# A new order of all engines for retention and a squared-ReLU MLP: other durations in the plan, and two casts moved to ScalarE

## The chip, the cores and the metric

The kernel runs on one core of one Trainium2 chip. The metric is the device time of one execution, in microseconds. The median of eight executions of the kernel before is 289.78 us (289.51 to 290.66).

## What is computed

```
scores = q @ k^T / 8                      # 8 batches, 8 heads, 576 positions, head size 64
Dmat[i, j] = gamma_h ** (i - j) if i >= j else 0,  gamma_h = 1 - 2 ** (-5 - h)
x = (scores * Dmat) @ v                   # retention; x as 4608 tokens x 512
out = relu(x @ w_in) ** 2 @ w_out         # w_in 512 x 2048, w_out 2048 x 512; float32 in and out
```

## The kernel before

**Units and groups.** The 4608 tokens are 36 units of 128. Units 0 to 7 are pairs: two neighbouring units are loaded together (tile `pair`, one transfer for each of k, q, v) and handled by `add_unit_pair` and `add_ret_pair`; the others by `add_unit` and the joined retention code. Two units make a group, and there are 18 groups, 0 to 17.

**Retention.** It is done chunk by chunk with a state R. For a pair, k and q are cast to 16 bits (`kx`, `qx`, line 424) and v is multiplied by decay factors (`vx`, line 420), each in two halves; TensorE transposes kx and qx (`psT`, line 439), ScalarE copies the result (`kqT`, line 450). Then come small 64 x 64 matmuls on TensorE (line 357): scores (`psc`), k times v (`psS`) and outputs (`psO`). VectorE masks the scores (`rx`, line 490; `rT`, line 692 for later units), steps the state (`stmp`, `R`, lines 514 and 461) and scales the output into the MLP's input (`xT`, lines 577 and 751). Later units are cast by GpSimd (`kq`, `v`, lines 371 to 387) and transposed by a DMA that SP issues (line 400). psO2 below is the psO of group 2.

**MLP.** For each group, eight blocks of `ph` (line 876, 256 columns, 8 matmuls a block); ScalarE takes the ReLU (`rl`, line 884); ScalarE or VectorE squares it (`gT`, lines 894 and 896). The second layer of groups 1 to 17 is a Strassen product: seven products p1 to p7 of eight matmuls (`po`, line 973) instead of eight, from sums of gT (`gS`, line 946, VectorE) and sums of w_out (`wT`, line 827, VectorE). p1 and p2 need gT alone; p7, p6, p5 and p3 need sums, called here by number: sum 3 for p7, sum 2 for p6 (made in two halves), sum 1 for p5, sum 4 for p3; p4 needs wT3 and gT. Products share banks, so ScalarE copies p1, u2 and u4 out between them (line 986) and VectorE adds into `o` (line 996). Group 0 uses the plain product with 512 columns (line 916).

**The weights** come in eight transfers that GpSimd issues with a cast on the way (w0 to w3 of w_in, w4 to w7 of w_out), between the loads of pairs 0 and 2 and those of pairs 4 and 6. Before the first MLP block, TensorE runs 34 junk matmuls (`warm`, line 256) where it has nothing else.

**What sets the order.** Nothing is ordered by hand. Each piece of work is a task with an engine, a key and a duration; `Schedule.emit` plays them against each other, and each engine takes the ready task with the lowest key. The order that comes out is the program; on the chip semaphores hold each instruction until its inputs are there. The planned durations and landings so decide only the order, not the times. Transfers are tasks too, with a landing time of `after` plus an entry of `LAG`.

The line numbers in the text are those of the kernel before.

Of the kernel before, what the change touches and what calls it, by code (L numbers as in the profile page):

```python
# [15 lines left out]
class Schedule:  # L16
# [4 lines left out]
        self.count = dict(count)  # L21
        self.tasks = []

    def add(self, eng, key, dur, fn, deps=(), acq=(), after=None, lag=0.0):
        t = dict(eng=eng, key=key, dur=dur, fn=fn, acq=acq, n=len(self.tasks), users=[], free=[], lag=lag,
                 left=len(deps), ready=0.0, lat=self.LAT[eng] if after is None else after)
        for d in deps:
            d["users"].append(t)
        self.tasks.append(t)
        return t  # L30
# [11 lines left out]
    def emit(self):  # L42
        ready = {e: [] for e in self.LAT}
        busy = {e: False for e in self.LAT}
        events = []
        order = []
        seq = 0

        def push(at, what, t):
            nonlocal seq  # L50
            seq += 1
            heapq.heappush(events, (at, seq, what, t))
        for t in self.tasks:
            if t["left"] == 0:
                heapq.heappush(ready[t["eng"]], (t["key"], t["n"], t))
        now = 0.0
        while True:
            for e in ready:
                if busy[e]:
                    continue  # L60
                held = []
                while ready[e]:
                    item = heapq.heappop(ready[e])
                    t = item[2]
                    if all(self.count[r] >= t["acq"].count(r) for r in t["acq"]):
                        for r in t["acq"]:
                            self.count[r] -= 1
                        t["start"] = now
                        order.append(t)
                        busy[e] = True  # L70
                        push(now + t["dur"], "end", t)
                        break
                    held.append(item)
                for item in held:
                    heapq.heappush(ready[e], item)
            if not events:
                break
            now = events[0][0]
            while events and events[0][0] <= now + 1e-9:
                _, _, what, t = heapq.heappop(events)  # L80
                if what == "end":
                    busy[t["eng"]] = False
                    for w in t["users"]:

                        push(now + (0.0 if w["eng"] == t["eng"] else t["lat"]), "dep", w)
                    for g in t["free"]:
                        push(now + t["lat"], "free", g)
                elif what == "dep":
                    t["left"] -= 1
                    if t["left"] == 0:  # L90
                        push(now + t["lag"], "go", t)
                elif what == "go":
                    heapq.heappush(ready[t["eng"]], (t["key"], t["n"], t))
                else:
                    t["left"] -= 1
                    if t["left"] == 0:
                        self.count[t["res"]] += 1
        assert len(order) == len(self.tasks)
        for t in order:
            t["fn"]()  # L100
# [3 lines left out]
def kernel(  # L104
# [114 lines left out]
    for hp in range(NP):  # L219
# [2 lines left out]
    nc.scalar.activation(out=dec128, in_=lnrow_R, func=ACTF.Exp, scale=128.0)  # L222

    L = 2 * NF
    WARM = 34
    EARLY = 20
    SQ_ACT = (0, 1, 2, 3, 4, 5, 6)
    SPREAD = 0.1
    QL = 0.8
    BESIDE = 1.1  # L230
    PAUSE = 1.5
    PARTS = 1
    WT_KEY = 96
    URGENT = 40
    SQ_LATE = (1, 4, 6)
    JOIN = 5
    LAG = {"k4": 0.7, "q4": 0.5}
    LAG_T, LAG_O = 1.5, 5.0
    PAIRED = 8
    FIRST = ["k0", "q0", "v0", "k2", "q2", "v2", "w0", "w1", "w2", "w3", "w4", "w5", "w6", "w7", "k4", "q4", "v4", "k6", "q6", "v6"]  # L240
# [1 line left out]
                          R=5, Rm=2, kqT=6))  # L242
    add = sched.add
# [28 lines left out]
        nc.gpsimd.tensor_copy(out=iota_pt[0:64], in_=iota_p[0:64])  # L272
        nc.gpsimd.tensor_scalar(out=iota_pt[64:128], in0=iota_p[64:128], scalar1=-64.0, scalar2=None, op0=ALU.add)

    tail_pool = add_gated("POOL", 4, "v", 2.2, make_tail_pool)
    tail_dec = add("DVE", 0, 0.3, lambda: make_vdec("tail", tile_of["iota_pt"]), deps=[tail_pool])

    def dma_task(key, dur, fn, **kw):
# [46 lines left out]
    def add_weight(i):  # L325
        fb = i % 4

        def fn():
            src, dst = ((w_in[:, fb * 512:(fb + 1) * 512].rearrange("(m p) f -> p m f", p=P), w_in16[:, :, fb * 512:(fb + 1) * 512]) if i < 4 else
                        (w_out[fb * 512:(fb + 1) * 512, :].rearrange("(n p) m -> p n m", p=P), w_out16[:, fb * 4:(fb + 1) * 4, :]))  # L330
            tile_of["w", i] = nc.gpsimd.dma_start(out=dst, in_=src)  # L331
            if i == 0:
                behind(tile_of["w", i], tile_of["load", "v", 0])
        issue = add("POOL", -90 + i, 0.9, fn, deps=issues[-1:] or [loaded["v", 0]], lag=1.0 if issues else 0.0)
        issues.append(issue)
        t = add("SP", 0, 2.75, lambda: None, deps=last_load + [issue], after=2.1 + LAG.get(f"w{i}", 0.0))
        last_load[:] = [t]
        wcast[i] = [t]

# [63 lines left out]
    def add_unit_pair(u, base):  # L403
# [4 lines left out]
        for i, name in enumerate("kqv"):  # L408
            xs[name] = []
            for e in range(2):  # L410
                eng = ("DVE" if (e if name == "v" else lead) else "ACT" if name == "k" and u >= 4 or u == 2 and e else
                       "DVE" if name == "q" and u == 2 else "POOL")

                def fc(name=name, e=e, eng=eng):
                    if (name + "x", u) not in tile_of:
                        tile_of[name + "x", u] = cast.tile([P, 2, H * D], FP16, name=name + "x", tag="kq16")
                    t = tile_of[name + "x", u][:, e]
                    x = tile_of[name + "32", u][:, :, e * D:(e + 1) * D]
                    if name == "v":
                        (nc.vector if eng == "DVE" else nc.gpsimd).tensor_tensor(  # L420
                            out=t.rearrange("p (h d) -> p h d", d=D), in0=x,
                            in1=vdec[f"pair{e}"].rearrange("p (h o) -> p h o", o=1).to_broadcast([P, H, D]), op=ALU.mult)
                    else:
                        engines[eng](out=t.rearrange("p (n b a d) -> p n b a d", n=2, b=2, a=2),
                                     in_=x.rearrange("p (a n b) d -> p n b a d", n=2, a=2))
                dur = (dict(POOL=1.1, DVE=0.6) if name == "v" else dict(POOL=0.62, DVE=0.4, ACT=0.59))[eng]
                xs[name].append(add(eng, base + (7 if name == "v" else i + e / 2), dur, fc, deps=[loaded[name, u]],
                                    acq=() if e else ("kq",)))
            if xs[name][0]["eng"] == xs[name][1]["eng"]:
                sched.need(xs[name][1], xs[name][0])  # L430
# [270 lines left out]
    def after_sums(g, t, key, res):  # L701
# [21 lines left out]
        if not c0:  # L723
            T["Rread", g - 1].append(r0)
        r1 = add("DVE", key + 0.2 - URGENT, 0.69, fr1, deps=[r0])
        r2 = add("DVE", key + 0.3, 0.65, fr2, deps=[r1], acq=("R",))
        T["Rm", g], T["R", g], T["Rread", g], T["Rmread", g] = r0, r2, [], r1
        sched.free("ff", [r0])
        sched.free("ff", [r1])
# [92 lines left out]
    def add_wT(i, in0, in1):  # L822
        ts = []
        for h in range(2):
            def f(h=h):
                sl = slice(h * HF // 2, (h + 1) * HF // 2)
                nc.vector.tensor_tensor(out=wT[i][:, sl], in0=in0[:, sl], in1=in1[:, sl], op=ALU.subtract)
            ts.append(add("DVE", WT_KEY + i, 0.7, f, deps=sum((wcast[j] for j in range(4, 8 if i else 6)), [])))
        return ts

    t1 = add_wT(0, wB[0, 1], wB[0, 0])
# [1 line left out]
    t3 = add_wT(2, wB[1, 1], wB[0, 1])  # L833
    t4 = add_wT(3, wB[1, 0], wT[1])
    for x, y in ((t2, t1), (t4, t2)):
        for p in y:
            for w in x:
                sched.need(w, p)
    wT_done = {7: t3, 6: t2, 5: t1, 4: t4}

    def store(u, o, lo=0, hi=DM, engs=(nc.sync, nc.sync)):
# [16 lines left out]
    def add_ff(g):  # L858
# [10 lines left out]
        for fb in range(NF // nf):  # L869
# [18 lines left out]
            def fg(fb=fb, on_act=on_act):  # L888
# [5 lines left out]
                    nc.scalar.activation(out=t, in_=rl, func=ACTF.Square)  # L894
                else:
                    nc.vector.tensor_tensor(out=t, in0=rl, in1=rl, op=ALU.mult)  # L896
            r = add("ACT", place(4 * fb + 4), 0.6, fr, deps=[f1[-1]], acq=("rl",))
            sched.free("ff", [r])
            sq.append(add("ACT" if on_act else "DVE", place(4 * fb + 6), 0.63 if on_act else 0.55, fg, deps=[r] + sq[:1],
                          acq=() if fb else ("g",)))  # L900
            sched.free("rl", [sq[-1]])
        sched.free("x", [f1[-1]])
        base2 = base + NF * n
# [28 lines left out]
    def add_strassen(g, us, base, sq):  # L932
# [7 lines left out]
        def add_sum(k, key, parts, in0, in1, op, deps, start=()):  # L940
            out_ = []
            for h in range(parts):
                def f(sl=cut(parts, h)):
                    if ("S", g) not in tile_of:
                        tile_of["S", g] = stage.tile([P, 4, HF, P], FP16, name="gS", tag="wst")
                    nc.vector.tensor_tensor(out=tile_of["S", g][:, k, sl], in0=in0(sl), in1=in1(sl), op=op)  # L946
                out_.append(add("DVE", key + h, (BESIDE if h else 0.5) if parts > 1 else 0.8, f, deps=deps(h, parts) + list(start)))
            sums[k] = out_
            return out_
        nb = len(sq) // 2  # L950
# [161 lines left out]
```

## Time and profile before

| What | Value |
| --- | --- |
| profiled execution, its own time | 289.7 us |
| its span | 288.0 us |
| TensorE busy | 280.4 us (97%), 4346 matmuls |
| VectorE busy | 176.1 us (61%) |
| ScalarE busy | 187.6 us (65%) |
| GpSimd busy | 89.2 us (31%) |
| granted TensorE clock | 0.999 |
| share of TensorE in the chain that ended last | 91% |

A busy share is an average over the span. TensorE's rows are pipelined and their ends modelled: where two rows of one engine overlap, the starts are the firmer numbers, and the time that work took is read from start to start. Idle time of an engine that is not the bottleneck costs nothing.

### The profile page before, as it was taken

What the parts mean: (1) busy time and instruction counts of PE and PEld (TensorE: products, weight loads), DVE (VectorE), ACT (ScalarE), POOL (GpSimd) and SP (SyncE); (2) the same over time, 40 slices, a digit from 0 to 9 for tenths busy, and PEclk for the clock granted to TensorE, in tenths of its full rate; (3) what the DMA queues carried; (4) which work ended last, traced back from release to release, by engine and by line L of the source; (5) the groups of instructions that cost most, each with busy time, mean ns of one, the idle gap of its engine ahead of it and who ended that gap; (6) DMA issues with size and microseconds to landing.
All of it is one profiled execution on the core that took longest, in us unless ns stands there. A gap on an engine that the chain in (4) does not pass through costs nothing.

```text
span 288.0 us, 10135 instructions
## 1 busy us (share of the span) xinstructions
PE 280.4 (97%) x4346; PEld 235.9 (82%) x4346; DVE 176.1 (61%) x341; ACT 187.6 (65%) x363; POOL 89.2 (31%) x124
## 2 busy tenths in 40 slices
PE   6999999999999999999999999999999999999994
PEld 2568767888888888888888888888888888888883
DVE  4772389868566756647656564767565566364632
ACT  5558975667585857657576748675848675847830
POOL 5660035435524243433426151524434000000000
PEclk9999999999999999999999999999999999999999
DMA  7999999889998898989899997989889420102004
GB/s 200 276 208 207 247 292 269 162 235 161 219 223 172 217 207 206 182 209 163 222 150 231 205 196 166 210 201 238 185 195 210 96 77 2 73 2 75 0 4 144
DMA packets 122156, 49.94 MB, mean 173 GB/s; under 512 B 94720, under 2 KB 117760, under 8 KB 122112
## 3 DMA queue, kind: packets, MB, share of 16 engines
q1 hardware_dynamic: 117568, 44.84, 70.9%
q0 software_dynamic: 4224, 4.19, 8.8%
q8 instruction: 34, 0.56, 0.8%
q10 hardware_dynamic: 320, 0.26, 0.4%
q14 instruction: 10, 0.08, 0.1%
HBM read 36.70 MB, written 9.44 MB: 160 GB/s over the span
## 4 chain that ended last, share of the span: by engine, by line
PE 91%; DMA 3%; POOL 2%; issue 2%; DVE 0%; POOLq 0%; DVEq 0%
PE ph L876 44%; PE po L973 37%; PE psO L357 4%; DMA w_in<-in_moe_w_in_dram 3%; PE po L916 2%; PE psc L357 2%; PE psS L357 2%; PE psT L439 1%; POOL mask L216 0%; POOL vx L420 0%; POOL w_in L331 0%; DVE o L996 0%; POOL mask_full L208 0%; POOL mask_tail L208 0%; DVE p L1025 0%
## 5 line engine op out<-in xcount | busy, mean ns | idle before, releaser
L876 PE MATMUL ph<-xT,w_in 128*128 128x256 f16 x1152 | 136.6, 273 | 0.2 <-DMA w_in<-in_moe_w_in_dram 0.2
L876 PEld LDWEIGHTS <-w_in 128*128 128x128 f16 x1152 | 111.4, 98 | 14.6 <-DMA w_in<-in_moe_w_in_dram 0.5
L884 ACT ACTIVATE rl<-ph 128x512 f16<-128x512 f32 x144 | 84.3, 587 | 50.4 <-PE ph L876 47.8
L894 ACT ACTIVATE gT<-rl 128x512 f16<-128x512 f16 x118 | 74.4, 631 | 3.4
L973 PEld LDWEIGHTS <-gS 128*128 128x128 f16 x544 | 51.7, 98 | 6.5
L973 PE MATMUL po<-wT,gS 128*128 128x256 f16 x408 | 55.8, 273 | 0.0
L946 DVE TENSOR_TENSOR gS<-gT,gS 128x512 f16<-128x512 f16 (+1 forms) x51 | 30.7, 603 | 24.2 <-ACT gT L894 23.7
L973 PEld LDWEIGHTS <-gT 128*128 128x128 f16 x408 | 39.6, 98 | 4.9
L973 PE MATMUL po<-w_out,gT 128*128 128x256 f16 x272 | 36.7, 273 | 0.0
L387 POOL TENSOR_TENSOR v<-v,vdec_full 128x512 f16<-128x512 f32 x24 | 26.8, 1117 | 26.3 <-DMA v<-in_v_dram 13.8
L371 POOL CAST kq<-k 128x512 f16<-128x512 f32 x28 | 20.9, 748 | 35.0 <-DMA k<-in_k_dram 34.6
L946 DVE TENSOR_TENSOR gS<-gT 128x1024 f16<-128x1024 f16 x34 | 23.6, 695 | 7.0 <-ACT gT L894 6.9
L382 POOL CAST kq<-q 128x512 f16<-128x512 f32 x24 | 16.4, 685 | 32.7 <-DMA q<-in_q_dram 32.6
L896 DVE TENSOR_TENSOR gT<-rl 128x512 f16<-128x512 f16 x26 | 11.9, 457 | 20.7 <-ACT rl L884 20.7
L996 DVE TENSOR_TENSOR o<-po,u 128x256 f32<-128x256 f32 x33 | 13.9, 423 | 15.4 <-PE po L973 7.7
L986 ACT COPY u<-po 128x256 f32<-128x256 f32 x34 | 12.5, 369 | 15.8 <-PE po L973 15.7
L996 DVE TENSOR_TENSOR o<-po,p 128x256 f32<-128x256 f32 x18 | 7.6, 424 | 21.3 <-ACT u L986 13.4
L751 DVE TENSOR_TENSOR xT<-psO,gam_full 128x512 f16<-128x512 f32 x28 | 18.0, 685 | 4.0 <-PE psO L357 3.9
L973 PE MATMUL po<-w_out,gS 128*128 128x256 f16 x136 | 18.0, 273 | 0.0
L973 PE MATMUL po<-wT,gT 128*128 128x256 f16 x136 | 17.6, 273 | 0.0
L692 DVE TENSOR_TENSOR rT<-psc,mask_full 128x512 f16<-128x512 f32 x24 | 15.6, 685 | 3.1 <-PE psc L357 2.8
L461 DVE TENSOR_TENSOR R<-stmp,dec 128x512 f16<-128x512 f32 (+1 forms) x18 | 12.6, 702 | 0.5
(82 smaller groups left out, 219.9 us busy)
## 6 DMA issues: line engine op xcount, KB each, us to landing
out_dram<-o SPq DMA_DIRECT2D x32, 256.0 KB, 2.6
k<-in_k_dram SPq DMA_DIRECT2D x24, 256.0 KB, 4.3
q<-in_q_dram SPq DMA_DIRECT2D x96, 64.0 KB, 3.3
v<-in_v_dram SPq DMA_DIRECT2D x24, 256.0 KB, 3.4
pair<-in_k_dram SPq DMA_DIRECT2D x4, 512.0 KB, 7.1
pair<-in_q_dram SPq DMA_DIRECT2D x4, 512.0 KB, 7.3
pair<-in_v_dram SPq DMA_DIRECT2D x4, 512.0 KB, 6.9
w_in<-in_moe_w_in_dram POOLq DMA_DIRECT2D x4, 512.0 KB, 9.1
```

The source lines that it names most:

```text
L357: t = nc.tensor.matmul(out_, lhsT=lhsT, rhs=rhs, start=start, stop=True, skip_group_check=True, tile_position=(64 * row, 64 * col))
L371: op(out=out_.rearrange("p (n b a d) -> p n b a d", n=2, b=2, a=2), in_=in_.rearrange("p (a n b) d -> p n b a d", n=2, a=2))
L382: nc.gpsimd.tensor_copy(out=tile_of["kq", u][:, 1].rearrange("p (t a d) -> p a t d", t=4, a=2), in_=tile_of["q32", u].rearrange("p (a t) d ...
L387: nc.gpsimd.tensor_tensor(out=t, in0=tile_of["v32", u], in1=vdec[kind].rearrange("p (h o) -> p h o", o=1).to_broadcast([P, H, D]), op=ALU. ...
L692: tile_of["masking", g] = nc.vector.tensor_tensor(out=tile_of["rT", g][:, :, a], in0=tile_of["psc", g][a].rearrange("p (s n i) -> p s n i" ...
L751: nc.vector.tensor_tensor(out=tile_of["x", g].rearrange("p n (s e i) -> p e (n s) i", s=n, e=2)[:, c], in0=y.rearrange("p (o t r) -> p o r ...
L876: nc.tensor.matmul(tile_of["ph", g, fb][:, j, :], lhsT=w_in16[:, m, fi * P:(fi + 1) * P], rhs=tile_of["x", g][:, m, :], start=(m == 0), st ...
L884: nc.scalar.activation(out=t, in_=tile_of["ph", g, fb], func=ACTF.Relu)
L894: nc.scalar.activation(out=t, in_=rl, func=ACTF.Square)
L946: nc.vector.tensor_tensor(out=tile_of["S", g][:, k, sl], in0=in0(sl), in1=in1(sl), op=op)
L973: nc.tensor.matmul(tile_of["pb", g, bank], lhsT=left(i), rhs=right[:, i, :], start=(start and i == 0), stop=(i == HF - 1), skip_group_chec ...
L996: nc.vector.tensor_tensor(out=o_tile(u)[:, half * HM:(half + 1) * HM], in0=bank(x), in1=tile_of[name, g], op=ALU.add)
```

## The change

The planner learns that a VectorE task on 16-bit data (`soft`) advances at 0.22 of its rate while a GpSimd task of over 0.5 us runs, and such tasks get shorter durations of their own. Weight transfers and landings get other values, 26 junk matmuls are issued in place of 34, sums and squares of group 1 get a lower key (`HURRY`), each half of a weight sum waits only for its own transfer, the constants of the last, shorter chunks (`tail_pool`: two GpSimd operations, then one on VectorE and one on ScalarE) are tied to the v of unit 8 instead of unit 4, and all four casts of k and q of the second pair (units 2 and 3) go to ScalarE; two of them were there before, one was on GpSimd and one on VectorE. As the order is made anew, instructions trade places on every engine. No computation is changed.

```diff
+    SHARED = 0.22
...
+        def shared(beside):
+            t = port["task"]
+            if t is not None:
+                port["left"] -= (now - port["at"]) * (self.SHARED if port["beside"] else 1.0)
+                port["at"] = now
+                t["end"] = now + max(port["left"], 0.0) / (self.SHARED if beside else 1.0)
+                push(t["end"], "end", t)
+            port["beside"] = beside
...
+                        if e == "POOL" and t["dur"] > 0.5:
+                            shared(True)
...
-    WARM = 34
+    WARM = 26
...
-    BESIDE = 1.1
+    HURRY = 60
...
-    LAG = {"k4": 0.7, "q4": 0.5}
+    LAG = {"k0": 0.3, "q2": 0.1, "w7": 1.4, "k4": 0.3, "q4": 0.7, "v4": 0.6, "q6": 0.3, "v6": 1.0}
...
-    tail_pool = add_gated("POOL", 4, "v", 2.2, make_tail_pool)
+    tail_pool = add_gated("POOL", 8, "v", 0.45, make_tail_pool)
...
-        t = add("SP", 0, 2.75, lambda: None, deps=last_load + [issue], after=2.1 + LAG.get(f"w{i}", 0.0))
+        t = add("SP", 0, 2.58, lambda: None, deps=last_load + [issue], after=3.0 + LAG.get(f"w{i}", 0.0))
...
-                eng = ("DVE" if (e if name == "v" else lead) else "ACT" if name == "k" and u >= 4 or u == 2 and e else
-                       "DVE" if name == "q" and u == 2 else "POOL")
+                eng = ("DVE" if (e if name == "v" else lead) else "ACT" if name == "k" and u >= 4 or u == 2 and name != "v" else "POOL")
...
-        r2 = add("DVE", key + 0.3, 0.65, fr2, deps=[r1], acq=("R",))
+        r2 = add("DVE", key + 0.3, 0.62, fr2, deps=[r1], acq=("R",), soft=True)
...
-            ts.append(add("DVE", WT_KEY + i, 0.7, f, deps=sum((wcast[j] for j in range(4, 8 if i else 6)), [])))
+            ts.append(add("DVE", WT_KEY + i, 0.68, f, deps=wcast[4 + h] + (wcast[6 + h] if i else []), soft=True))
...
-            r = add("ACT", place(4 * fb + 4), 0.6, fr, deps=[f1[-1]], acq=("rl",))
+            r = add("ACT", place(4 * fb + 4) - HURRY * (g == 1 and fb == 7), 0.6, fr, deps=[f1[-1]], acq=("rl",))
...
-            sq.append(add("ACT" if on_act else "DVE", place(4 * fb + 6), 0.63 if on_act else 0.55, fg, deps=[r] + sq[:1],
-                          acq=() if fb else ("g",)))
+            sq.append(add("ACT" if on_act else "DVE", place(4 * fb + 6) - HURRY * (g == 1 and not on_act), 0.63 if on_act else 0.43, fg, deps=[r] + sq[:1],
+                          acq=() if fb else ("g",), soft=not on_act))
...
-                out_.append(add("DVE", key + h, (BESIDE if h else 0.5) if parts > 1 else 0.8, f, deps=deps(h, parts) + list(start)))
+                out_.append(add("DVE", key + h - HURRY * (g == 1), 0.43 if parts > 1 else 0.72, f, deps=deps(h, parts) + list(start), soft=True))
```

More of the change, by code (lines that the diff above doesn't have):

```diff
@@ L22, in __init__, with add @@
         self.tasks = []
-    def add(self, eng, key, dur, fn, deps=(), acq=(), after=None, lag=0.0):
-        t = dict(eng=eng, key=key, dur=dur, fn=fn, acq=acq, n=len(self.tasks), users=[], free=[], lag=lag,
+    SHARED = 0.22
+    def add(self, eng, key, dur, fn, deps=(), acq=(), after=None, lag=0.0, soft=False):
+        t = dict(soft=soft, eng=eng, key=key, dur=dur, fn=fn, acq=acq, n=len(self.tasks), users=[], free=[], lag=lag,
                  left=len(deps), ready=0.0, lat=self.LAT[eng] if after is None else after)
@@ L56, in emit @@
         now = 0.0
+        port = dict(task=None, left=0.0, at=0.0, beside=False)
+        def shared(beside):
[6 more added lines that the diff above has]
+            port["beside"] = beside
         while True:
@@ L70, in emit @@
                         busy[e] = True
-                        push(now + t["dur"], "end", t)
+                        t["end"] = now + t["dur"]
+                        if t["soft"]:
+                            port.update(task=t, left=t["dur"], at=now)
+                            shared(port["beside"])
+                        else:
+                            push(t["end"], "end", t)
+                        if e == "POOL" and t["dur"] > 0.5:
+                            shared(True)
                         break
@@ L81, in emit @@
                 if what == "end":
+                    if abs(t["end"] - now) > 1e-6:
+                        continue
+                    t["end"] = -1.0
                     busy[t["eng"]] = False
+                    if t["soft"]:
+                        port["task"] = None
+                    elif t["eng"] == "POOL" and t["dur"] > 0.5:
+                        shared(False)
                     for w in t["users"]:
@@ L835 @@
     for x, y in ((t2, t1), (t4, t2)):
-        for p in y:
-            for w in x:
-                sched.need(w, p)
+        for w, p in zip(x, y):
+            sched.need(w, p)
     wT_done = {7: t3, 6: t2, 5: t1, 4: t4}
```

## The prediction

> **What bounds the kernel now.** I read the stages first, then the timeline of the two stretches that the change rearranges. The stages (us; busy time of each engine with its instructions; the last columns are the granted clock, the share of the DMA engines and GB/s):
>
> ```profile
> core 0: us, PE busy (x) PEld busy (x) DVE busy (x) ACT busy (x) POOL busy (x), PEclk, DMA share, GB/s
> 0.00:17.40 17.40, 14.60 (x234) 7.67 (x234) 11.19 (x51) 8.58 (x19) 11.80 (x32) 1.00 1.03 232
> 17.40:41.00 23.60, 23.29 (x233) 17.23 (x223) 11.19 (x21) 19.43 (x35) 3.46 (x6) 1.00 1.22 237
> 41.00:56.00 15.00, 14.90 (x317) 12.06 (x314) 14.45 (x25) 9.28 (x20) 8.29 (x10) 1.00 0.97 236
> 56.00:259.00 203.00, 202.72 (x3358) 176.88 (x3351) 126.78 (x220) 136.23 (x263) 65.61 (x78) 1.00 0.82 173
> 259.00:288.00 29.00, 24.87 (x228) 22.04 (x226) 12.51 (x27) 14.04 (x29) 0.00 (x0) 0.99 0.18 55
> ```
>
> From 17.4 to 259 us TensorE is idle for 0.31 + 0.10 + 0.28 = 0.69 us. Both programs hold the same 1152 ph, 984 po and 2176 small matmuls (psT, psc, psS, psO). So a new order can win only those 0.69 us, a few waits hidden inside "busy" (below), or time ahead of 17.4. VectorE is busy 14.45 of 15.00 us between 41 and 56, the one stage where another engine is as full; the DMA engines are full up to about 46 us.
>
> The start, from the timeline (start, duration, idle time before and what ended it):
>
> ```profile
> 5.73 0.23 DVE L182 TENSOR_SCALAR vdl_tail<-lnrow,iota_pt 128x8 f32<-128x8 f32 x1 [2.55 <-POOL iota_pt L273]
> 5.87 0.76 DVE L424 CAST kx<-pair 128x512 f16<-128x512 f32 x2
> 6.65 0.76 DVE L424 CAST qx<-pair 128x512 f16<-128x512 f32 x2
> 11.62 0.63 POOL L424 CAST kx<-pair 128x512 f16<-128x512 f32 x1
> 17.49 1.92 PE L876 MATMUL ph<-xT,w_in 128*128 128x256 f16 x16
> 19.63 1.48 PE L876 MATMUL ph<-xT,w_in 128*128 128x256 f16 x12 [0.21 <-DMA w_in<-in_moe_w_in_dram]
> ```
>
> The first 16 ph matmuls use the first chunk of w_in, the next wait at 19.63 for the second chunk, which the chain of waits shows landing at 10.81 + 8.77 = 19.58. That landing starts the full stretch.
>
> The second set of pairs (units 4 to 7):
>
> ```profile
> 38.85 1.33 POOL L424 CAST qx<-pair 128x512 f16<-128x512 f32 x2 [19.68 <-DMA pair<-in_q_dram]
> 39.96 0.61 PE L439 MATMUL psT<-ident,kx 128*128 128x128 f16 x8
> 40.51 0.69 DVE L420 TENSOR_TENSOR vx<-pair,vdec_pair 128x512 f16<-128x512 f32 x1 [1.35 <-DMA pair<-in_v_dram]
> 40.65 1.45 POOL L420 TENSOR_TENSOR vx<-pair,vdec_pair 128x512 f16<-128x512 f32 x1 [0.47 <-PE psT L439]
> 42.91 0.45 PE L357 MATMUL psS<-vx,kx 64*64 64x64 f16 x32
> 44.05 0.64 PE L357 MATMUL psc<-kqT 64*64 64x128 f16 x32
> 48.98 0.66 PE L357 MATMUL psS<-vx,kx 64*64 64x64 f16 x32
> 50.32 0.59 PE L357 MATMUL psc<-kqT 64*64 64x128 f16 x16
> ```
>
> GpSimd's q casts start as q4 lands and its v product as v4 lands. The psS at 48.98 takes 0.66 where the one at 42.91 takes 0.45: 0.21 us of waiting for vx (VectorE, 48.49 + 0.68). Sixteen psc take 0.59 where 32 take 0.64: some 0.17 us of waiting.
>
> **The start: nothing.** The constants of the tail leave the head of the VectorE queue, so kx of pair 0 can be cast about 1 us before 5.87. The qx casts start at 6.65 because q lands then, and they come before psT, psc and all that follows: no gain. Pair 2's kx goes from GpSimd (11.62 + 0.63 = 12.25) to ScalarE (two by 0.62 from 10.28: 11.52), so psT comes up to 0.7 us earlier; its q cast leaves VectorE (0.42) for ScalarE (0.62), which is idle there. GpSimd's third w_in issue moves up past that cast, into a DMA queue that is full anyway. The last small matmuls before ph now end before the weights are there: ph begins some 0.3 us earlier, at best about 17.15, does its 16 x 0.109 = 1.75 us by 18.9, and waits for 19.58 all the same. psO1 now stands 8 matmuls earlier in that stretch (about 20.16); its masks ended at 19.80 and depend on the same psS, so no wait. Sum zero, hidden by the landing; a gain would need an earlier landing.
>
> The 8 warm-up matmuls that go (34 to 26) only filled waits. The trace grants 1.00 of the clock in spite of a 1.11 us gap before the first psT; the gaps that I expect now stay under 1 us: zero. The Trainium skill ("TensorE: Matmul & The Clock Gate", Part 1, The HAM clock gate) speaks against removing such fill: an idle window of about 3.4 us halves the clock until a busy one has passed. By that page one such window would cost some 1.7 us, and the sum would be 291.9; no gap here comes near it, and no run here shows the limit.
>
> **Second set of pairs, the wait.** The new order puts psT of k4 nine 512-wide matmuls earlier: 39.96 - 9 x 0.217 = 38.0, about when its kx is cast (ScalarE, two by 0.57, as soon as k4 lands, which the trace does not show). psT of q4 follows after 0.45 + 6 x 0.217: 39.8. But q4's casts end at 38.85 + 1.33 = 40.18, and the landing cannot move, since the DMA engines are full before it: about 0.4 us of waiting. Then 0.45 + 3 x 0.217 + 6 x 0.109 + 0.1 bring psS to 42.05, and vx ends at 40.65 + 1.45 = 42.10: psS at about 42.12. Before, psS stood at 42.91 with 12 more matmuls behind it (8 of p1, 8 of p7, 2 of p6, against 6 of p1); without those, 42.91 - 12 x 0.109 = 41.60. The new order is 0.52 behind at the same work. Bounds: 0 if GpSimd's casts were done when TensorE arrives; 0.6 if k4's cast is late too. I take 0.5, from GpSimd's rows.
>
> **More visits.** Each change from wide matmuls to small ones and back costs TensorE a bubble. psc 4 and 5, one visit before, become two; psO2 with psc6 becomes two. Start to start, less the wide matmuls between: 32 psc cost 44.62 - (43.29 + 6 x 0.109) = 0.67; 16 alone, 50.85 - (49.56 + 6 x 0.109) = 0.63, less the 0.17 wait, 0.46. Two halves cost 0.92: +0.25. psO2 with psc6 costs 48.65 - (46.83 + 4 x 0.109) = 1.38; psO alone is some 1.09 (13.35 to 14.41 and its entry), with 0.46 for psc: +0.17. Together +0.4, bounds 0.2 and 0.5. From group 4 on both orders make the same visits.
>
> **Waits that go.** In the new order VectorE multiplies vx of pair 6 before TensorE needs it (its queue, from 41.2: three sums 2.2, R 0.4, four masks 2.5, two state steps 0.9, vx 0.7: 47.9; psS comes at about 48.5), and psc7 comes a ph block later: -0.21 and -0.17. In group 2 the last product waited 0.12 us for VectorE's o (70.95); its distance is now covered: -0.1.
>
> **Moved without cost.** The tail's constants (GpSimd 0.18 + 0.22, VectorE 0.23, ScalarE 0.30) now follow GpSimd's v product of unit 8. Behind VectorE's wait are queued o (the last product of group 1 needs it), a state step, R and two masks (psO3 needs them). By the old rows, v at 50.13 + 1.04 and the two ops end at 51.6, where VectorE arrives at about 51.3: 0.3 lost there, masks done at 54.5, psO3 due at 55.0 (55.32, a ph block of 0.87 earlier in the order, and 0.5 behind). Cover 0.5; if gone, the excess falls on TensorE. On SP, stores and loads trade places; transposes landed 1.9 us or more before their psc (83.28 against 85.2).
> In groups 2 to 15 the sums are placed by other durations. The tightest is group 15: from the last ph to the second half of product 6 were 4.07 us (250.37 to 254.44) and are now 28 x 0.109 = 3.06, as psO17 moves behind; the sum was done 2.53 after (252.48 + 0.42). Slack 0.5; the same count leaves 0.6 to 1 in groups 4, 5, 9, 10 and 11. I take zero, with an upper bound in the second rival.
>
> **Sum.** 0.5 + 0.4 - 0.21 - 0.17 - 0.1 = +0.4. The profiled execution took 289.7 (span 288.0 and 1.7 around it), 0.08 under the median of 289.78: 290.1 for it, 290.2 for the median. A measurement of this kernel can tell about 0.2%, 0.58 us: 289.2 and 290.36 are the limits of "same".
>
> **Rivals.**
> 1. The forecast, +0.4, chance 0.62; its bounds run from +0.1 to +0.8, and about 0.17 of the chance lies above +0.58.
> 2. Slower: sums come late at product 6 in steady state. VectorE's 16-bit sums take 0.42 alone and up to 0.92 beside GpSimd, and the decay R took 1.52 at 68.30 beside a v product, against 0.69; groups 4 and 5 now have their first S2 sum behind such an R. It decides where the stretch exceeds the 0.5 to 0.7 of slack. Three of those joints over by 0.3 each: +0.9, 291.1. Against it: the old order had such stretches and TensorE lost 0.28 in 203 us. Chance 0.22.
> 3. The wait for q4 does not come (casts shorter than 0.66, or TensorE later): -0.1, 289.7. For it: two free GpSimd casts would be 1.25. Chance 0.11.
> 4. Faster: w_in lands earlier, the only way past the floor, and must do so by 1 us. Against it: a full DMA queue with the same bytes ahead. 289.0, chance 0.05.
>
> Within 0.2%: 0.45 + 0.11 = 0.56; slower 0.17 + 0.22 = 0.39; faster 0.05. The range takes in case 3 with 0.2 to spare and case 2: 289.5 to 291.1.
>
> **What would show it.** Right: ph waits near 19.6 as before and longer (about 0.7); psT of q4 starts as GpSimd's casts end, near 40.2; two more visits between 41 and 56; no wait at the second psS; 56 to 259 with as little idle time as before. Wrong: the second w_in chunk landing before 19; p6 matmuls waiting for gS; VectorE held at vdl_tail beyond 52; a granted clock below 0.99 before 20 us.

## The result and the profile after

The changed kernel is slower by 0.43%: 290.91 us median of 11 runs (290.13 to 291.94) against 289.70 us of 32 runs of the kernel before on the same chip (289.22 to 290.66), ratio 1.0043, 95% interval 1.0032 to 1.0053. The range on record, 289.5 to 291.1, holds it; the likeliest single case, +0.4 us and within 0.2%, is too small by 0.8 us.

The profiled execution of the changed kernel took 290.67 us (span 288.9), 0.97 more than that of before, at a granted clock of 1.000. The stages of the kernel after, cut as before (the last columns are the granted clock, the share of the DMA engines and GB/s):

```profile
core 0: us, PE busy (x) PEld busy (x) DVE busy (x) ACT busy (x) POOL busy (x), PEclk, DMA share, GB/s
0.00:17.40 17.40, 13.17 (x223) 7.05 (x223) 10.57 (x48) 9.22 (x20) 10.55 (x29) 1.00 1.03 232
17.40:41.00 23.60, 23.20 (x227) 17.23 (x228) 11.79 (x21) 19.93 (x36) 3.54 (x6) 1.00 1.22 237
41.00:56.00 15.00, 14.49 (x309) 11.21 (x311) 14.19 (x26) 8.67 (x19) 8.37 (x12) 1.00 0.95 230
56.00:259.00 203.00, 202.58 (x3349) 176.81 (x3350) 130.47 (x221) 135.44 (x263) 63.81 (x78) 1.00 0.84 174
```

From 17.4 to 259 us TensorE is idle 0.40 + 0.51 + 0.42 = 1.33 us instead of 0.69. The first stage looks worse than it costs, 13.17 busy instead of 14.60: most of that is junk matmuls that are gone and waits that they had filled.

Idle time misses the bubbles inside "busy", so the account is made at equal work: every matmul gets its steady price (0.109 us for a ph or po of 256 columns, 0.056 for a psT, 0.012 for a small one), and the two traces are compared where the same sum has been started. After minus before:

| Stretch (us of before) | After minus before |
| --- | --- |
| up to 20: second chunk of w_in lands at 19.76 instead of 19.58 | +0.18 |
| 20 to 108: second set of pairs and group 2 | +0.36 |
| 108 to 137: psc13 and psc14 wait for transposes | +0.68 |
| 137 to the end: one visit at 155 us cheaper by 0.17 | -0.17 |
| end of TensorE's work | +1.05 |

The second set of pairs, from the timeline of the kernel after (L450 casts, L446 is the v product, L384 the small matmuls; here and below, lines of the kernel after stand some 25 lines further down):

```profile
38.90 1.17 POOL L450 CAST qx<-pair 128x512 f16<-128x512 f32 x2 [19.44 <-PE psT L465]
39.94 0.61 PE L465 MATMUL psT<-ident,qx 128*128 128x128 f16 x8
40.68 1.45 POOL L446 TENSOR_TENSOR vx<-pair,vdec_pair 128x512 f16<-128x512 f32 x1 [0.61 <-ACT gT L919]
41.03 0.82 PE L998 MATMUL po<-w_out,gT 128*128 128x256 f16 x6
42.18 0.45 PE L384 MATMUL psS<-vx,kx 64*64 64x64 f16 x32 [0.33 <-POOL vx L446]
42.56 0.39 PE L998 MATMUL po<-w_out,gT 128*128 128x256 f16 x2
...
43.10 0.42 PE L384 MATMUL psc<-kqT 64*64 64x128 f16 x16
43.45 0.39 PE L998 MATMUL po<-wT,gS 128*128 128x256 f16 x2
43.77 0.42 PE L384 MATMUL psc<-kqT 64*64 64x128 f16 x16
44.12 1.49 PE L998 MATMUL po<-wT,gS 128*128 128x256 f16 x12
...
48.69 0.45 PE L384 MATMUL psS<-vx,kx 64*64 64x64 f16 x32
49.07 0.39 PE L998 MATMUL po<-wT,gS 128*128 128x256 f16 x2
```

The first psS waits for GpSimd's vx, which ends at 42.13: start to start, less the wide matmuls, that visit takes 42.56 - (41.03 + 6 x 0.109) = 0.88 us against 0.47 for the same 32 psS at 48.69. The two lone visits of psc take 0.44 and 0.45. The second psS no longer waits.

The transposes, from the timeline of SP's queue, where the second row belongs to psc13 (first the kernel after, then the one before):

```profile
115.67 2.73 SPq L427 DMA_TRANSPOSE kqT<-kq  x1
119.44 1.23 SPq L427 DMA_TRANSPOSE kqT<-kq  x1
```

```profile
114.11 1.94 SPq L400 DMA_TRANSPOSE kqT<-kq  x1
117.37 1.92 SPq L400 DMA_TRANSPOSE kqT<-kq  x1
```

The later one is issued 2.1 us later than before and lands at 123.05 instead of 121.78, while psc13 now starts at 122.65 instead of 124.66. For each visit of psc, the landing of its second transpose and the margin up to the start of that visit:

| Visit | Before: landed, psc starts, margin | After: landed, psc starts, margin |
| --- | --- | --- |
| psc10 | 83.28, 85.52, 2.24 | 83.36, 84.31, 0.95 |
| psc11 | 95.74, 98.36, 2.62 | 97.49, 97.59, 0.10 |
| psc12 | 108.52, 111.64, 3.12 | 111.01, 110.87, -0.14 |
| psc13 | 121.78, 124.66, 2.88 | 123.05, 122.65, -0.40 |
| psc14 | 135.41, 136.12, 0.71 | 137.04, 136.61, -0.43 |

(The second transpose is needed half a visit after its start, so a small negative margin can still be met.)

At psc13 the wait stands inside a row: the same 32 matmuls, first after and then before.

```profile
122.65 0.76 PE L384 MATMUL psc<-kqT 64*64 64x64 f16 x32
```

```profile
124.66 0.43 PE L357 MATMUL psc<-kqT 64*64 64x64 f16 x32
```

The profiled execution can't show one thing: the twelve executions whose clock is on record fall into two kinds. Five had a mean granted clock of 0.999 or 1.000 and took 290.66 in the median; six had 0.994 or less and took 291.15; one had 0.997.

### The profile page after: what moved, and what is told of

Its sections match the earlier page's. It is cut to its first block, busy times and chain, and to the rows that moved or that the text cites. A ratio compares the mean times of both kernels' runs of the same rounds, so it can differ in the third digit from the quotient of the medians.

```text
span 288.9 us, 10117 instructions
## 1 busy us (share of the span) xinstructions
PE 279.4 (97%) x4338; PEld 235.3 (81%) x4338; DVE 179.6 (62%) x340; ACT 188.2 (65%) x365; POOL 86.3 (30%) x123
## 4 chain that ended last, share of the span: by engine, by line
PE 70%; DMA 15%; SPq 5%; DVE 3%; ACT 2%; POOL 2%; issue 1%; POOLq 0%; DVEq 0%; ACTq 0%
PE ph L901 32%; PE po L998 31%; DMA w_out<-in_moe_w_out_dram 4%; PE psO L384 3%; DMA q<-in_q_dram 3%; DMA pair<-in_v_dram 3%; DMA pair<-in_k_dram 2%; DMA kqT<-kq 2%; SPq L325 2%; SPq L343 2%; PE psc L384 2%; PE psS L384 2%; SPq L328 1%; POOL vx L446 1%; ACT rl L909 1%
## 5 line engine op out<-in xcount | busy, mean ns | idle before, releaser
L971 DVE TENSOR_TENSOR gS<-gT,gS 128x512 f16<-128x512 f16 (+1 forms) x51 | 31.9, 626 | 20.0 <-ACT gT L919 19.5
L414 POOL TENSOR_TENSOR v<-v,vdec_full 128x512 f16<-128x512 f32 x24 | 26.2, 1090 | 27.6 <-DMA v<-in_v_dram 18.1
L971 DVE TENSOR_TENSOR gS<-gT 128x1024 f16<-128x1024 f16 x34 | 25.9, 761 | 8.2 <-ACT gT L919 8.1
L398 POOL CAST kq<-k 128x512 f16<-128x512 f32 x28 | 20.0, 713 | 35.8 <-DMA k<-in_k_dram 35.0
L487 DVE TENSOR_TENSOR R<-stmp,dec 128x512 f16<-128x512 f32 (+1 forms) x18 | 13.5, 751 | 0.5
```

The lines of the kernel that those rows point to most:

```text
L398: op(out=out_.rearrange("p (n b a d) -> p n b a d", n=2, b=2, a=2), in_=in_.rearrange("p (a n b) d -> p n b a d", n=2, a=2))
L414: nc.gpsimd.tensor_tensor(out=t, in0=tile_of["v32", u], in1=vdec[kind].rearrange("p (h o) -> p h o", o=1).to_broadcast([P, H, D]), op=ALU. ...
```

## The experiments

Each kernel was timed against runs of the kernel before on its own chip; ratios are to those. Theory: four things make the loss, the early psS, the extra visits, the late transposes and, in some executions, a lost clock. Rivals stand with each run.

**1 and 2. The junk matmuls, in both directions.**

```diff
-    WARM = 26
+    WARM = 34        # after_warm34; before_warm26 is the kernel before with the opposite edit
```

> The kernel after with 34 junk matmuls instead of 26; nothing else in the order changes (two visits of fill come back before psS1 and psc2, one grows before psO0). Theory A: the removed fill lets the granted TensorE clock fall to half for one window in some executions (the timed executions of the kernel after show a mean granted clock of 0.991 to 1.000, and those below 0.995 are about 0.7 us longer). Then every execution here shows 0.998 or more and the median falls by about 0.5, to 290.4. Theory B: the clock differs by chance or by chip; then the clocks stay mixed and the median stays at 290.9. Under both, the profiled span without a fall of the clock stays at 288.9 within 0.2.

> The kernel before with 26 junk matmuls instead of 34; nothing else in the order changes (the fill before psO0, psS1 and psc2 goes). Theory A (fill holds the clock): some executions show a mean granted clock near 0.994 and are about 0.7 us longer, median 290.1 to 290.5. Theory B (the clock differs by chance): same as before, 289.7, clocks as before.

after_warm34: 290.87 us, 1.0032 (1.0011 to 1.0052), all twelve executions at a clock of 0.999 or 1.000. before_warm26: 290.86, 1.0019 (0.9995 to 1.0044), four of twelve at 0.994 or 0.991. So the clock goes with the number of junk matmuls and not with the order. The median of after_warm34 did not fall to that of before, 290.39 on this chip, nor to the 290.4 expected: the order has its own loss. Its trace, of an execution that took 291.88 us, is 2.3 us behind at equal work, 1.2 of it in waits for transposes (at 98.1, 123.5 and 138.0 us) and 0.7 in waits for weights to land (at 25.0 and 30.8 us).

**3. The landing of v4 later in the plan.**

```diff
-    LAG = {..., "v4": 0.6, ...}
+    LAG = {..., "v4": 1.2, ...}
```

> The kernel after with the planner's landing of v4 0.6 us later (LAG of v4 1.2 instead of 0.6): psS2 stands 4 wide matmuls later and psO2 is joined with psc6 again; the order of the groups behind changes as well. Theory: the wait of psS2 for vx (0.40 us) goes and one visit less saves 0.17; by the profile 0.5 to 0.6 faster than the kernel after, 290.3. Rival: TensorE only arrives later at the next full point and the time is kept, or the new order behind it waits elsewhere: 290.9 or more.

293.68 us, 1.0125 (1.0103 to 1.0147). The psS wait goes, but the new plan puts VectorE's `o` of group 1 behind the tail's constants at a worse moment. From its timeline:

```profile
52.05 0.23 DVE L209 TENSOR_SCALAR vdl_tail<-lnrow,iota_pt 128x8 f32<-128x8 f32 x1 [2.45 <-POOL iota_pt L300]
52.19 0.42 DVE L1021 TENSOR_TENSOR o<-po,u 128x256 f32<-128x256 f32 x1
...
52.66 0.57 PE L998 MATMUL po<-wT,gT 128*128 128x256 f16 x2 [1.60 <-DVE o L1021]
```

and from its stages, the clock around that wait:

```profile
49.20:52.60 3.40, 1.86 (x29) 1.24 (x27) 0.95 (x4) 0.65 (x3) 2.48 (x5) 1.00 0.86 175
52.60:56.10 3.50, 3.44 (x17) 2.38 (x17) 3.47 (x9) 0.28 (x2) 1.16 (x3) 0.52 0.95 231
```

VectorE stands 2.45 us at vdl_tail, p4 waits 1.60 us for `o`, and over the next 3.5 us the granted clock is 0.52. At equal work the stretch from 45 to 54 us costs 3.1 us.

**4. The same order with the constants tied to unit 4 again.**

```diff
-    tail_pool = add_gated("POOL", 8, "v", 0.45, make_tail_pool)
+    tail_pool = add_gated("POOL", 4, "v", 2.2, make_tail_pool)      # on top of after_v4
```

> The later landing of v4 in the plan (v4 1.2, the order of after_v4, which ran 293.7 us) with the constants of the tail tied to unit 4 again; TensorE's order is the same as in after_v4. Theory (VectorE stood 2.45 us at vdl_tail, waiting for GpSimd's iota_pt, and o and p4 behind it; the clock then fell to 0.50 for 3.4 us): the wait of 1.6 us at p4 and the halved clock near 53 to 56 go together, 1.6 + 1.7 = 3.3 us less than after_v4, about 290.4. Rival (o waits for something else, such as the sums ahead of it, and the clock fell for another reason): less than 0.8 us of it comes back and a stretch of clock below 0.9 stays near 53.

The wait and the low clock near 53 are gone: the stretch from 45 to 54 us now costs 0.4 us less than before instead of 3.1 more. The cause of that wait is shown. The time came out at 292.80 (1.0092, 1.0056 to 1.0128), not at 290.4: the profiled execution lost 1.2 us to a halved clock from 17.4 us on and 3.8 us near 97, where psc11 waited 2.00 us for a transpose and the clock fell to 0.50 again from 99 to 102.

**5. The changed kernel once more**, without an edit.

> The changed kernel itself once more, beside the next three on the same chip. Theory: about 1.004 times the kernel before; some half of the executions at a mean granted clock of 0.994 to 0.997 and 0.8 us longer than the others; in the profile psS of units 4 and 5 waits about 0.4 us for GpSimd's vx near 42.2, and psc13 or psc14 waits up to 0.4 us for transposed kqT near 122 and 137. Rival (the order alone, the clock is chance of one chip): the same ratio with every execution at 0.999 or above.

290.70 us, 1.0028 (1.0007 to 1.0049); three of twelve executions at 0.994. At equal work, psc12 lost 0.28 us in this execution and psc13 and psc14 0.15 together, so how late the transposes are differs from one execution to the next. The loss from 20 to 108 us was there again (+0.40), but not where it was expected: TensorE lost 0.38 us at 30.5, waiting for w_out to land, and so came to psS at 42.09, when vx was done (42.02), with no wait left.

**6. The early psS alone, two wide matmuls later.** On every other engine the instructions stand as in the changed kernel.

```diff
-        t = add("PE", base + 4.5, 0.5, fk, deps=T["kvx", u], acq=("ff", "ff"))
+        t = add("PE", base + 4.5, 0.5, fk, deps=T["kvx", u], acq=("ff", "ff"), lag=0.4 if u == 4 else 0.0)
```

> Only the psS of units 4 and 5 comes two 256-column matmuls later; the instructions of all other engines stand as in the changed kernel. Theory (TensorE arrives too early for GpSimd's vx, ready near 42.13): the wait of 0.40 falls to about 0.18, 0.22 us less than the changed kernel on this chip. Rival (the whole stretch is short of work, since sum 3 on VectorE now stands behind vx and ends near 42.41): the time comes back as a wait of the first p7 matmuls for gS, and nothing is gained.

291.08 us, 1.0038 (1.0021 to 1.0055): by the medians nothing is gained, 0.2 us is less than they tell apart. What this run brought is a trace of an execution with the clock at 0.994 (TensorE's busy time is the second number of a row, the clock the third from the end):

```profile
14.00:17.40 3.40, 1.78 (x75) 1.42 (x73) 2.88 (x6) 1.65 (x4) 3.07 (x4) 0.99 1.24 208
17.40:20.70 3.30, 3.27 (x18) 2.23 (x19) 3.07 (x6) 1.06 (x2) 2.11 (x3) 0.50 1.24 206
```

The low clock sits where ph begins. At 18.7 us of before, this execution is 1.30 us behind, the traces of the other kernels with a clock of 1.00 there by 0.13 to 0.26: one such fall costs about 1.1 us. The wait for the second chunk of w_in, which the profiled execution of the changed kernel has at that place, is gone: it hides the rest. The same 3.4 us ahead of it, without a fall, first the kernel before and then the changed one:

```profile
14.00:17.40 3.40, 3.28 (x86) 2.00 (x82) 3.08 (x7) 1.17 (x3) 3.40 (x4) 1.00 1.24 207
```

```profile
14.00:17.40 3.40, 1.72 (x73) 1.40 (x73) 2.93 (x6) 1.58 (x4) 3.12 (x4) 1.00 1.24 208
```

With 34 junk matmuls TensorE is busy 3.28 of these 3.40 us, with 26 it is 1.72.

So 1.72 went unpunished in one execution where 1.78 did not in another. What decides is where the windows begin. At the start the matmuls come at half their later rate (junk matmuls 0.427 us apart, then 0.216); the clock rises at 5.36 us in the trace of the changed kernel, at 7.12 in after_s4, 4.93 in after_v4 and 7.13 in after_v4_tail4. Counted from there in steps of 3.413 us, the falls of these traces ahead of the end of the work come after 3.00 steps (after_s4, 17.36 us), 14.00 (after_v4, 52.71), and 3.00 and 27.00 (after_v4_tail4, 17.37 and 99.29). In the step just before these four falls TensorE was busy 1.84, 1.81, 1.72 and 1.42 us; in every other such step up to the end of its work, in all fourteen traces, 2.00 us or more, and no fall followed. First the step before the fall in after_s4, then the two steps of the changed kernel that share its thin stretch between them:

```profile
13.94:17.36 3.42, 1.84 (x77) 1.42 (x73) 2.84 (x6) 1.71 (x4) 3.03 (x4) 1.00 1.24 207
```

```profile
12.19:15.60 3.41, 2.63 (x60) 1.83 (x58) 2.76 (x6) 2.77 (x6) 1.79 (x2) 1.00 1.25 236
15.60:19.01 3.41, 2.22 (x75) 1.87 (x75) 3.08 (x7) 0.50 (x2) 3.41 (x6) 1.00 1.23 203
```

An estimate from this: if the steps may begin anywhere, 36 to 41% of their positions put a step of under 1.84 us busy into the four traces with 26 junk matmuls and a steady clock (the changed kernel twice, after_lag_t, before_warm26), and none does in a trace with 34. Counted over all executions of the five kernels with 26, below, it is 24 of 60.

**7. The same with 34 junk matmuls.** 

```diff
-    WARM = 26
+    WARM = 34        # on top of after_s4
```

> After_s4 with 34 junk matmuls instead of 26. Theory (26 are too few to hold the clock in every execution): no execution below 0.999 and a median about 0.4 us (half of the executions by 0.8) below that of after_s4, some 1.002 times the kernel before. Rival (the page's limit of 3.4 us of idleness is nowhere near, fill costs and brings nothing): the same median and the same spread of clocks as after_s4.

290.56 us, 1.0021 (1.0003 to 1.0038), 0.52 under after_s4 on the same chip; no execution below 0.997 where after_s4 had six of twelve at 0.994 or less. The psS wait in its trace is down to 0.2 us at equal work, as expected; the trace is 0.56 us behind that of before. By 54 us of before, after_s4 is only 0.8 us behind this trace of the same order with the clock kept: TensorE, late by the fall, found vx ready there (psS at 43.11, vx done at 42.20).

**8 and 9. The scores of the groups with late transposes put later.**

```diff
-                     acq=("prO", "prS", "ff", "ff", "ff", "ff"))
+                     acq=("prO", "prS", "ff", "ff", "ff", "ff"), lag=1.2 if g in (8, 9) else 0.0)        # after_lag_t
+                     acq=("prO", "prS", "ff", "ff", "ff", "ff"), lag=1.2 if g in (6, 7, 8, 9) else 0.0)  # after_s4_w34_t4, on top of after_s4_w34
```

> The kernel after with psc13 and psc14 held back 1.2 us in the plan (a lag on those two tasks), so that they stand 0.9 to 1.3 us later in TensorE's order. Theory: their waits for the transposes (0.33 and 0.29 us in the profile) go, 0.6 faster than the kernel after: 290.3. Rival: the waits are for something that moves along (psS8 or the next group's psc wait instead): 290.9.

> After_s4_w34 with the scores of groups 8 to 11 (psc11 to psc14, counted in visits) put 0.4 to 1.3 us later in TensorE's order, nothing else. Theory (in the changed order the transposes of these groups land later than TensorE asks for them, by another amount in each execution): no wait for kqT over 0.1 us between 95 and 140 us, and a median 0.2 to 0.5 us under after_s4_w34: 1.0005 to 1.0015 times the kernel before. Rival (the waits only move to the next product, as the same bytes pass the same queue): other waits of the same sum between 95 and 160 us and the ratio of after_s4_w34, 1.002.

after_lag_t: 291.26, 1.0030 (1.0011 to 1.0049). after_s4_w34_t4: 290.71, 1.0014 (0.9999 to 1.0029). The waits became fewer but did not go: in the first trace psc11, which was not moved, waited 1.4 us; in the second psc14, moved by only 0.4 us, waited 1.05. A fixed margin on some of the groups doesn't cover what varies. That these waits are what is left was expected and is seen; that they can be bought off by placing psc a little later is not shown.

**10. One part alone: the casts on ScalarE.**

```diff
-                eng = (... "ACT" if name == "k" and u >= 4 or u == 2 and e else
-                       "DVE" if name == "q" and u == 2 else "POOL")
+                eng = (... "ACT" if name == "k" and u >= 4 or u == 2 and name != "v" else "POOL")
```

> One part alone: the kernel before with all four casts of the second pair on ScalarE. Up to the second block of ph, TensorE's order differs in the place of four junk matmuls; psO1 stands four ph matmuls earlier. Theory (the start is hidden by the second chunk of w_in, landing near 19.6): no difference, 0.999 to 1.001 times the kernel before, ph beginning up to 0.3 us earlier and waiting longer near 19.6. Rival (the casts are what the small matmuls of the start wait for): the end of the start stretch moves with them, 0.3 us or more gained.

289.83 us against 289.97, 0.9984 (0.9969 to 0.9998). ph began 0.23 us later (17.72 against 17.49) and not earlier, as in before_land (17.74), which leaves the casts where they were. At equal work the trace is within 0.1 us of before from 24 to 125 us, then psc14 waits 0.4 us for a transpose. No loss by this part; the gain of 0.16% is under what the measurement can tell, and the trace doesn't show where it would come from. Of all kernels run here it is the only one whose interval lies under 1.

**11. One part alone: the landings.**

```diff
-    LAG = {"k4": 0.7, "q4": 0.5}
+    LAG = {"k0": 0.3, "q2": 0.1, "w7": 1.4, "k4": 0.3, "q4": 0.7, "v4": 0.6, "q6": 0.3, "v6": 1.0}
...
-        t = add("SP", 0, 2.75, lambda: None, deps=last_load + [issue], after=2.1 + LAG.get(f"w{i}", 0.0))
+        t = add("SP", 0, 2.58, lambda: None, deps=last_load + [issue], after=3.0 + LAG.get(f"w{i}", 0.0))
```

> One part alone: the kernel before with the new landings of the loads and the new duration and landing of the weights, 34 junk matmuls and no other edit. TensorE's order of the second set of pairs up to its first psS comes out as in the changed kernel. Theory (the landings alone place that psS ahead of GpSimd's vx): psS waits 0.3 to 0.45 us near 42.2, as in the changed kernel, and the stretch 38 to 58 us costs 0.3 to 0.6 us more than before; every execution at 0.997 or above. Rival (the VectorE durations, HURRY or the moved constants make the wait): no wait over 0.1 us there.

292.32 us (292.27 without one execution of 295.22), 1.0066 (1.0042 to 1.0090), by its median more than the whole change costs. From its timeline:

```profile
40.21 0.40 PE L439 MATMUL psT<-ident,qx 128*128 128x128 f16 x4
40.77 0.40 PE L439 MATMUL psT<-ident,qx 128*128 128x128 f16 x4 [0.16 <-POOL qx L424]
...
111.53 0.32 PE L357 MATMUL psc<-kqT 64*64 64x64 f16 x16 [1.47 <-DMA kqT<-kq]
...
125.11 0.32 PE L357 MATMUL psc<-kqT 64*64 64x64 f16 x16 [0.81 <-DMA kqT<-kq]
```

Here GpSimd's two q casts took 1.66 us, and psT of q4 waited for them (0.3 us more than its work), the form that the prediction gave the wait; psS behind it then found vx ready. So the place expected here, psS, was wrong and the size was not: up to 42 us this cost 0.6 us against the kernel before, and with a wait of 0.46 us for a copy of u at 50 us the whole stretch cost 1.0, more than expected. Two transposes were late, by 1.47 and 0.81 us.

**12. The other way round: everything but the landings.** 

```diff
-    WARM = 26
+    WARM = 34
-    LAG = {"k0": 0.3, "q2": 0.1, "w7": 1.4, "k4": 0.3, "q4": 0.7, "v4": 0.6, "q6": 0.3, "v6": 1.0}
+    LAG = {"k4": 0.7, "q4": 0.5}
...
-        t = add("SP", 0, 2.58, lambda: None, deps=last_load + [issue], after=3.0 + LAG.get(f"w{i}", 0.0))
+        t = add("SP", 0, 2.75, lambda: None, deps=last_load + [issue], after=2.1 + LAG.get(f"w{i}", 0.0))
```

> One part undone: the changed kernel with the old landings of the loads and the old duration and landing of the weights, and with 34 junk matmuls; what stays are VectorE's durations beside GpSimd, HURRY, the moved constants and the casts of the second pair on ScalarE. Theory (the landings place the second pairs' psS ahead of vx and the scores of groups 8 to 11 ahead of their transposes): no wait over 0.1 us at the psS near 43, psc4 and psc5 in one visit again, and 0.9985 to 1.0015 times the kernel before. Rival (the new VectorE durations bring their own loss, sums late at product 6 or p4 late behind the moved constants): waits of 0.3 us or more for gS or o between 46 and 160 us, and 1.002 or more.

289.75 us against 290.17, 0.9998 (0.9975 to 1.0020). From its timeline:

```profile
43.69 0.45 PE L384 MATMUL psS<-vx,kx 64*64 64x64 f16 x32
43.96 0.62 PE L384 MATMUL psc<-kqT 64*64 64x128 f16 x32
```

psS comes 1.4 us after vx is done and the 32 psc follow in the same visit. At equal work this trace is 0.3 us ahead of before at 108 us; at 128 it loses 0.56 in one visit of small matmuls whose releaser the profile doesn't name. The loss of the change is thus in the landings and the junk matmuls; VectorE's durations, HURRY, the moved constants and the casts together cost nothing that can be measured, within an interval of 0.25% down and 0.20% up.

## Why the prediction was right or wrong

**The wait of the second pairs, +0.5: right in size, wrong in the input that ends it.** Measured 0.41 at psS. The prediction let psT of q4 wait for GpSimd's casts by their row of 1.33 us; they took 1.17 and psT passed at 39.94. GpSimd's vx ended at 42.13 against 42.10 predicted, and psS started at 42.18 against 42.12. In before_land the casts took 1.66 and the wait came at psT as predicted. Either way the arrival of pair 4 and GpSimd's work on it set the floor. In after_same TensorE lost the time ahead of it and psS waited no more; the sum up to 108 us came out the same.

**More visits, +0.4: right.** 0.44 + 0.45 for the two psc visits against 0.92 predicted and 0.67 before. psO2 with psc6 took 1.16 + 0.45 against 1.38 before, +0.23 for a predicted +0.17.

**Waits that go, -0.48: right where it can be read.** The second psS lost its 0.2 us, psc7 takes 0.44 instead of 0.64, and p4 of group 2 lost its wait (0.11 at equal work). The three terms sum to +0.4; the stretch from 20 to 108 us measured +0.36.

**Sums at product 6, zero: right.** No p6 matmul waits for gS in the trace of the change; the smallest distance left was 0.29 us, in group 4. The second rival is false: 56 to 259 us lost time, but to transposes.

**The tail's constants, zero with a cover of 0.5: right here, and the risk that it named is real.** In the changed kernel VectorE stands 0.57 us at vdl_tail and TensorE loses nothing. In after_v4, where VectorE arrives 1.6 us earlier (49.60 against 51.21), the excess falls on TensorE, 1.60 us.

**SP's trades, zero: wrong, +0.68 in the profiled execution.** The step took its margin, "1.9 us or more", from one visit (83.28 against 85.2). The table above has 0.71 for psc14 already in the kernel before, and the new order takes 0.8 to 2.0 us off the starts of psc10 to psc13 while the transposes land 0.1 to 2.5 us later. Order and landing have to be read for every visit, and the landing has a spread: of the traces, that of the changed kernel lost 0.68 us here, that of its repetition 0.4, that of before_land 2.6. This is the largest missed term of the profiled execution.

**The junk matmuls, zero: wrong; the clock fell in some four executions of ten.** Of 60 executions with 26 (the changed kernel twice, after_s4, after_lag_t, before_warm26), 24 had a clock of 0.994 or less; of 72 with 34 (experiments 1 and 7, after_s4_w34_t4, and 10 to 12) none was below 0.997, and of the 104 of the kernel before that were timed beside them two had 0.994 or less, at 294.16 and 296.33 us, which one such fall does not explain. The step compared the longest single gap, 1.0 us, with the length of a window. The traces say that it is the share: four windows with 1.42 to 1.84 of 3.41 us busy were each followed by a fall, those with 2.00 and more were not, and the longest gaps in after_s4 were 0.86 and 0.71. The profiled execution of the changed kernel kept its clock by luck of where its windows began. A fall costs about 1.1 us where it happens; less of it reaches the end. Falling executions of the changed kernel took 0.5 us more than steady ones (291.15 against 290.66), those of after_s4 no more (291.06 against 291.09 in the median). The median of the changed kernel, where both kinds mix, is 0.25 us above that of its steady executions; the intervals of 1 and 7 are too wide to show so little.

The Trainium skill ("TensorE: Matmul & The Clock Gate", Part 1, The HAM clock gate) was weighed there and set aside. It also states that the window of 3413 ns is free-running, so that where it falls differs from run to run. This agrees with the steps of 3.413 us in the traces, with the same order falling in some executions and not in others, and with the 3.4 us at 0.50. The prediction's estimate of 1.7 us, worked out from that page, is an upper end of the 1.1 measured. Its wording that the clock falls after an idle window does not fit: no trace here shows TensorE idle for more than 2.0 us before such a fall, and windows half busy were enough.

**Start, zero: right but for the clock.** The second chunk of w_in ended the wait, 0.18 us later than in the trace of before; in the other traces with a clock of 1.00 the same place is 0.01 to 0.12 late, 0.11 in after_same with the same order, so none of it is shown to belong to the order. That ph would begin earlier, at 17.15 at best, was wrong: it began at 17.84. psS waited 0.88 us for GpSimd's vx of pair 2, until 15.78, and psc another 1.01 us for something that the profile doesn't name, so the wait for the second chunk was 0.05 us and not 0.7. The landing hid this too.

The sum of the order from 20 to 108 us was right within 0.1 us. What made the result slower than the likeliest case were two terms set to zero, each from one row that was taken for the whole: a margin from one visit, and a limit compared with one gap. That the range holds the result is in part luck: its upper end was set for late sums at product 6, which did not come.

## What to carry to other kernels

An order that asks for an input sooner must be held against the landing of every such input, with its spread from execution to execution, because a planner with a sharper landing time spends exactly the margin that hid that spread. Filler work on TensorE is judged by the busy share of every stretch of some 3.4 us that it leaves, wherever the stretch begins, not by the longest gap, and by several executions, because one profile may show a clock of 1.00 by luck. When a new plan trades several things at once, undoing one input of the planner (here the landings) finds the loss faster than mending its symptoms one by one.

## What was not expected of the hardware

- The granted clock fell to 0.50 for 3.4 us after a window of 3.41 us in which TensorE was busy 1.84 us or less, with no single gap over 0.9 us (after_s4) and 1.6 us (after_v4). Windows of 2.00 us and more kept 1.00, in before_land even one with a wait of 1.47 us in it (2.20 us busy from 107.86 to 111.27). The windows follow one another from the first rise of the clock on, at another place in each execution.
- A transpose that SP issues takes 3.1 to 6.1 us from issue to landing in these traces, and its issue alone 1.2 to 3.7 us (1.23 and 2.73 in the rows above); the next load in the queue is issued behind it (at 118.45 us in the changed kernel, after 115.67 + 2.73 = 118.40).
- GpSimd's two q casts of 128 x 512 for pair 4 took from 1.16 us (after_same) to 1.72 us (after_oldland) in different traces for the same work.
